# Feed-forward blocks of 512 tokens in (n2, n1) order in place of 376-token blocks, with the mixing stages placed to deadlines

## The chip, the cores and the metric

One core of a Trainium2 chip runs the kernel. The metric is the device time of the program in microseconds (us). The kernel before takes 980.5 us (three runs, 980.26 to 980.66).

Ratios are the mean time of one kernel's runs over that of the other's runs of the same rounds, so they are not quite the ratio of the medians that are quoted.

## The reference

```python
def _attn_ref(x, filt_r, filt_i):            # x: 8 batches x 3008 positions x 256 channels
    X = np.fft.rfft(x, axis=1)
    Y = X * (filt_r + 1j * filt_i)[None]
    return np.fft.irfft(Y, n=x.shape[1], axis=1)

def _moe_ref(x, w_gate, w_val, w_out):       # x: 24064 tokens x 256; d_ff = 1536
    return (np.maximum(x @ w_gate, 0.0) * (x @ w_val)) @ w_out
```

The output is the second function applied to the first, with the eight batches laid end to end. The row of the output for position s of batch b is 3008 b + s.

## The kernel before

The Fourier transform of length 3008 = 94 x 32 is done in stages. A position is s = 32 n1 + n2, with n1 below 94 and n2 below 32. Per batch, 16 **items of A** transform over n1 (matmuls psA, then a write to memory, Abuf, and a gather into `at`). 14 **items of B** transform over n2, multiply by the filter and transform back over n2 (psX, products tt and uu, psD, then a write to Dbuf and a load into dC). **Item C** (psY) finishes the inverse over n1 and yields yT, the input of the feed-forward. A and B of batch b + 1 are woven one by one into the feed-forward of batch b.

```python
    def items_b(b, junk=0):
        def fwd(g):
            psX = ps.tile([128, 2, D], FP32, tag=fft_tag(), name="psX")
            ...                                   # 2 matmuls
            nc.vector.tensor_tensor(tt, psX, Ftr[:, g:g + 2, :], op=ALU.mult)
            ...                                   # uu likewise, from psX and Fti
        def inv():
            psD = ps.tile([128, 2, D], FP32, tag=fft_tag(), name="psD")
            ...                                   # 4 matmuls
            nc.scalar.copy(st["dsb"][:, o:o + 2, :], psD)
        ...                                       # one item: fwd of one pair, inv of an earlier one

    def item_c(b, z, h):
        psY = ps.tile([128, W], FP32, tag=fft_tag(), name="psY")      # W = 376
        for j in range(4):
            nc.tensor.matmul(psY[:, j * N1:(j + 1) * N1],
                             dCs[b, z][:, j, h * 128:(h + 1) * 128], M1, start=True, stop=True)
        dst = yTs[b, z][:, h]
        src = psY.rearrange("p (b a) -> p a b", a=N1)
        ...                                       # copy: ScalarE for h == 0, VectorE for h == 1

    def gv(blk, ft, prods):                       # gate and value of 128 of the 1536 features
        ...                                       # 4 matmuls of W columns into psV and psG
        nc.scalar.copy(vsb, psV[:, :W])
        nc.vector.scalar_tensor_tensor(prod, in0=psG[:, :W], scalar=0.0, in1=vsb,
                                       op0=ALU.max, op1=ALU.mult)

    def o_part(blk, s, prods):                    # output tiles of 128, 128 and 120 tokens
        ...                                       # 3 matmuls of 256 columns, psO
        if s in (7, 11):
            n = 2 if s == 7 else 1
            osb = fs.tile([128, 2, D], FP32, tag="osb", bufs=3)
            nc.scalar.copy(osb[:tw, :n], psO[:tw, :n])
            r0 = b * S + (t + 1 - n) * 128 * NZ + z
            nc.sync.dma_start(_ap(out, r0 * D, [[NZ * D, tw], [128 * NZ * D, n], [1, D]]),
                              osb[:tw, :n])
    ...
    turn["tags"] = ("fft",)                       # psA, psX, psD, psY share ONE tag: 2 psum tiles
    for bi, blk in enumerate(blocks):             # 64 blocks: batch b, group z of four n2
        ...                                       # A from step 5 (20 in batch 0), B from step 35 (51), every 2nd
        for ft in range(NFT):                     # 12 "steps" of a block
            gv(blk, ft, prods)
            if prev is not None:
                o_part(prev[0], ft, prev[1])
            for f in side.get(z * NFT + ft, ()):  # the items of A and B, loads
                f()
            if ft in (6, 10) and bi + 1 < len(blocks):
                item_c(*blocks[bi + 1], 0 if ft == 6 else 1)
```

Psum is the memory that the matmuls write. The kernel keeps eight tiles in it: two each for psV, psG and psO, and two for the tag `fft`.

## Time and profile before

| | before |
|---|---|
| time, median of 3 | 980.53 us |
| span of the profiled run | 978.5 us |
| TensorE (PE) busy | 960.5 us, 98% |
| feed-forward stretch: first psV to the end of the last output matmul | 60.7 to 974.9 us |
| PE waits within that stretch | 0.7 us |

From the page of the kernel before: busy time of each engine, then groups of instructions (line, engine, what it writes and reads, shape, count, then busy us, mean ns of one, idle us before them and what ended it) and output transfers (count, KB each, us from issue to landing).

```profile
span 978.5 us, 18320 instructions
...
PE 960.5 (98%) x6814; PEld 663.3 (68%) x6816; DVE 577.1 (59%) x1046; ACT 556.6 (57%) x1191; POOL 51.4 (5%) x85
...
L365 PE MATMUL psO<-WoT,prod 128*128 128x256 bf16 (+1 forms) x2304 | 375.0, 273 | 0.0
L345 PE MATMUL psV<-yT,WvT 128*128 128x376 bf16 x1536 | 370.4, 322 | 0.7 <-ACT yT L334 0.4
...
L328 PE MATMUL psY<-M_90,dC 96*128 96x94 bf16 x512 | 42.3, 204 | 0.0
...
out_dram<-osb SPq DMA_DIRECT2D x64, 256.0 KB, 2.3
...
out_dram<-osb SPq DMA_DIRECT2D x64, 120.0 KB, 1.9
```

The waits of PE inside the feed-forward stretch (total us, times, longest), all of them:

```profile
PE psV L345 <- ACT yT L334: 0.4, 1, 0.4
PE psV L345 <- DVE yT L336: 0.3, 1, 0.3
```

And the stretch view: length, then busy us of PE, its weight loads, VectorE, ScalarE, GpSimd, then granted clock and DMA.

```profile
60.70:974.90 914.20, 913.84 (x6608) 641.08 (x6607) 549.68 (x1000) 535.46 (x1154) 22.19 (x43) 1.00 0.37 102
```

So PE is never free for 914 us. The mean of 322 ns for a matmul is not its cost, since matmuls overlap. The cost is the distance from one start to the next. By the chain of waits it is 159.3 ns for 376 columns, 109.2 for 256 and 42.0 for 94, which is columns / 2.4 GHz plus 2.5 ns.

I take the twelfth of a block as a step, measure from its first psO matmul to the next step's, and subtract the sum of its matmuls at those costs. In the kernel before, no step is more than 0.2 us over that sum. This is worked out from the starts of the instructions in the trace, and I call it the excess of a step.

### The profile page before, as it was taken

How to read it: one execution, taken by the hardware profiler on the slowest of the kernel's cores; microseconds unless marked ns; L12 is line 12 of the kernel's file. 1: busy time of each engine (PE TensorE's matmuls, PEld its weight loads, DVE VectorE, ACT ScalarE, POOL GpSimd, SP SyncE). 2: the span in 40 equal slices, each digit the busy share in tenths (PEclk: the TensorE clock that was granted, in tenths of full speed). 3: DMA queues.
4: the chain of work that ended last, by engine and by line, in shares of the span. 5: the costliest groups of instructions: out<-in, count | busy, mean ns of one | idle time of the engine just before them, and what ended most of it. 6: DMA issues, size and time to landing. Idle time of an engine off the chain costs nothing.

```text
span 978.5 us, 18320 instructions
## 1 busy us (share of the span) xinstructions
PE 960.5 (98%) x6814; PEld 663.3 (68%) x6816; DVE 577.1 (59%) x1046; ACT 556.6 (57%) x1191; POOL 51.4 (5%) x85
## 2 busy tenths in 40 slices
PE   8699999999999999999999999999999999999998
PEld 2355677667775677757776577765777567777776
DVE  4543486448753586536854378543875449655554
ACT  3245666555655565555655556555665555655554
POOL 4520000000000000000000100001000000000000
PEclk9899999999999999999999999999999999999999
DMA  9993824192413814155231652318332241411111
GB/s 263 211 258 106 228 61 119 49 246 68 132 38 101 203 52 130 32 160 147 76 114 32 172 137 84 97 44 226 83 108 65 64 114 54 129 33 33 32 33 48
DMA packets 96825, 107.20 MB, mean 110 GB/s; under 512 B 6212, under 2 KB 85508, under 8 KB 95108
## 3 DMA queue, kind: packets, MB, share of 16 engines
q1 hardware_dynamic: 87760, 78.97, 29.1%
q0 software_dynamic: 8576, 25.86, 10.4%
q8 instruction: 53, 0.87, 0.4%
q10 hardware_dynamic: 400, 1.20, 0.3%
q14 instruction: 36, 0.29, 0.1%
HBM read 59.31 MB, written 49.81 MB: 112 GB/s over the span
## 4 chain that ended last, share of the span: by engine, by line
PE 95%; DMA 3%; POOL 1%; DVE 0%; ACT 0%; issue 0%; POOLq 0%; ACTq 0%
PE psO L365 26%; PE psV L345 25%; PE psG L345 25%; PE psA L243 11%; PE psY L328 2%; PE psX L274 2%; PE psD L294 2%; PE psD L293 2%; PE psJ L382 1%; DMA XF_89<-in_x_dram 1%; DMA at<-Abuf_71 1%; DMA XF_88<-in_x_dram 1%; DMA Abuf_71<-asb 1%; POOL uu L281 0%; DVE tt L277 0%
## 5 line engine op out<-in xcount | busy, mean ns | idle before, releaser
L350 DVE SCALAR_TENSOR_TENSOR prod<-psG,vsb 128x376 bf16<-128x376 f32 x768 | 421.4, 550 | 357.4 <-ACT vsb L348 348.3
L348 ACT CAST vsb<-psV 128x376 bf16<-128x376 f32 x768 | 363.5, 473 | 210.0 <-PE psV L345 209.3
L365 PE MATMUL psO<-WoT,prod 128*128 128x256 bf16 (+1 forms) x2304 | 375.0, 273 | 0.0
L345 PE MATMUL psV<-yT,WvT 128*128 128x376 bf16 x1536 | 370.4, 322 | 0.7 <-ACT yT L334 0.4
L345 PE MATMUL psG<-yT,WgT 128*128 128x376 bf16 x1536 | 369.8, 322 | 0.0
L365 PEld LDWEIGHTS <-prod 128*128 128x128 bf16 (+1 forms) x2304 | 246.1, 110 | 89.9
L345 PEld LDWEIGHTS <-WgT 128*128 128x128 bf16 x1536 | 149.7, 97 | 95.7 <-issue 0.9
L345 PEld LDWEIGHTS <-WvT 128*128 128x128 bf16 x1536 | 143.2, 98 | 66.9 <-issue 54.9
L246 ACT CAST asb<-psA 96x512 bf16<-96x512 f32 x128 | 74.4, 582 | 101.6 <-PE psA L243 100.5
L296 ACT CAST dsb<-psD 128x512 bf16<-128x512 f32 x96 | 56.0, 587 | 50.1 <-PE psD L294 48.7
L370 ACT COPY osb<-psO 128x512 f32<-128x512 f32 (+1 forms) x128 | 61.6, 481 | 19.9 <-PE psO L365 13.9
L277 DVE TENSOR_TENSOR tt<-psX,Ftr 128x512 bf16<-128x512 f32 x96 | 65.4, 682 | 10.4 <-PE psX L274 10.3
L243 PE MATMUL psA<-XF_89,WA 128*96 128x512 f32 x128 | 65.0, 592 | 1.4 <-DMA XF_89<-in_x_dram 1.4
L243 PE MATMUL psA<-XF_88,WA 128*96 128x512 f32 x128 | 65.1, 593 | 0.5 <-DMA XF_88<-in_x_dram 0.5
L283 DVE TENSOR_TENSOR uu<-psX,Fti 128x512 bf16<-128x512 f32 x90 | 61.3, 681 | 0.0
L294 PE MATMUL psD<-uu,I2u 128*128 128x256 bf16 x192 | 47.4, 274 | 2.9 <-POOL uu L281 2.8
L293 PE MATMUL psD<-tt,I2t 128*128 128x256 bf16 x192 | 47.7, 274 | 0.0
L328 PEld LDWEIGHTS <-dC 96*128 96x128 bf16 x512 | 35.8, 97 | 14.8 <-issue 12.0
L274 PE MATMUL psX<-at,F_91 128*128 128x256 bf16 x192 | 37.4, 277 | 6.4 <-DMA at<-Abuf_71 6.4
L328 PE MATMUL psY<-M_90,dC 96*128 96x94 bf16 x512 | 42.3, 204 | 0.0
L336 DVE CAST yT<-psY 128x376 bf16<-128x376 f32 x64 | 34.6, 541 | 12.5 <-PE psY L328 12.5
L334 ACT CAST yT<-psY 128x376 bf16<-128x376 f32 x64 | 30.2, 472 | 20.0 <-PE psY L328 20.0
(47 smaller groups left out, 201.3 us busy)
## 6 DMA issues: line engine op xcount, KB each, us to landing
out_dram<-osb SPq DMA_DIRECT2D x64, 256.0 KB, 2.3
XF_88<-in_x_dram POOLq DMA_DIRECT2D x20, 512.0 KB, 7.2
XF_89<-in_x_dram POOLq DMA_DIRECT2D x20, 512.0 KB, 6.5
out_dram<-osb SPq DMA_DIRECT2D x64, 120.0 KB, 1.9
XF_88<-in_x_dram SPq DMA_DIRECT2D x6, 256.0 KB, 5.2
XF_89<-in_x_dram SPq DMA_DIRECT2D x3, 512.0 KB, 8.1
Abuf_71<-asb SPq DMA_DIRECT2D x4, 384.0 KB, 5.3
at<-Abuf_71 SPq DMA_DIRECT2D x4, 384.0 KB, 6.1
```

What stands on the lines that cost most here:

```text
L243: nc.tensor.matmul(psA[0:NROW], WA[:, :NROW], XF[c * NC2 // NX2][:, o:o + 512], start=True, stop=True)
L246: nc.scalar.copy(dst, psA[0:NROW])
L277: nc.vector.tensor_tensor(tt, psX, Ftr[:, g:g + 2, :], op=ALU.mult)
L283: nc.vector.tensor_tensor(uu, psX, Fti[:, g:g + 2, :], op=ALU.mult)
L293: nc.tensor.matmul(psD[:, i], I2t[:, g + i, :], tt[:, i], start=True, stop=False)
L294: nc.tensor.matmul(psD[:, i], I2u[:, g + i, :], uu[:, i], start=False, stop=True)
L328: nc.tensor.matmul(psY[:, j * N1:(j + 1) * N1], dCs[b, z][:, j, h * 128:(h + 1) * 128], M1, start=True, stop=True)
L345: nc.tensor.matmul(pt[:, :W], w[:, h, ft * 128:(ft + 1) * 128], yt[:, h, :], start=(h == 0), stop=(h == 1))
L348: nc.scalar.copy(vsb, psV[:, :W])
L350: nc.vector.scalar_tensor_tensor(prod, in0=psG[:, :W], scalar=0.0, in1=vsb, op0=ALU.max, op1=ALU.mult)
L365: nc.tensor.matmul(psO[:tw, t % 2], prods[ft][:, t * 128:t * 128 + tw], WoT[:, ft, :], start=(ft == 0), stop=(ft == NFT - 1))
L370: nc.scalar.copy(osb[:tw, :n], psO[:tw, :n])
```

## The change

The intent: with matmuls of 512 columns, a width that psA already has, 47 blocks of 512 tokens pay the 2.5 ns less often than 64 of 376, and all output tiles are full ones (2,256 output matmuls instead of 2,304). As 3008 is no multiple of 512, blocks cross batches and tokens are taken in the order n2, then n1. A batch now lasts about 70 steps instead of 96, and A, B and C are placed backward from the step at which a block first needs the batch.

```diff
-    W = S // NZ
+    W = 512
+    NB = B * S // W
...
+    def runs(t, n):                               # pieces of n tokens within one n2
+        o = 0
+        while o < n:
+            b, r = divmod(t + o, S)
+            n2, n1 = divmod(r, N1)
+            w = min(N1 - n1, n - o)
+            yield o, b, n2, n1, w
+            o += w
...
-        for j in range(4):
-            nc.tensor.matmul(psY[:, j * N1:(j + 1) * N1], ...
+        for (o, b, n2, n1, w) in runs(k * W, W):
+            nc.tensor.matmul(psY[:, o:o + w],
+                             dCs[b, n2 // 4][:, n2 % 4, h * 128:(h + 1) * 128], M1[:, n1:n1 + w],
+                             start=True, stop=True)
...
-            nc.sync.dma_start(_ap(out, r0 * D, [[NZ * D, tw], [128 * NZ * D, n], [1, D]]),
-                              osb[:tw, :n])
+            for tt in range(t0, t + 1):
+                for (o, b, n2, n1, w) in runs(blk * W + tt * 128, 128):
+                    nc.sync.dma_start(_ap(out, (b * S + n1 * N2 + n2) * D, [[N2 * D, w], [1, D]]),
+                                      osb[o:o + w, tt % 2])
...
+    LAST = 9
+    for b in range(1, B):
+        end = (b * S // W - 1) * NFT + LAST - 5
+        if b == 1:
+            s0, sb0 = 13, 33
+            every = [sb0 + i + i // 2 for i in range(14)]
+        else:
+            s0 = end - 54
+            every = [(s0 + 24 | 1) + 2 * i for i in range(14)]
+        for i, f in enumerate(items_a(b)):
+            at_step(s0 + i, f)
+        for c in range(4):
+            at_step(s0 + 6 + 4 * c, lambda b=b, c=c: load_at(b, c))
+        ...
+        for i, f in zip(every, items_b(b)):
+            at_step(i, f)
+        at_step(every[-1] + 1, lambda b=b: load_d(b))
...
-            if ft in (6, 10) and bi + 1 < len(blocks):
-                item_c(*blocks[bi + 1], 0 if ft == 6 else 1)
+            if ft in (LAST - 2, LAST + 1) and k + 1 < NB:
+                item_c(k + 1, 0 if ft < LAST else 1)
```

The permutation of n2 in the tables of the inverse is dropped with the old order, and the last block evicts its output tile by tile.

More of the change, by code (lines that the diff above doesn't have):

```diff
@@ L53, in _tables @@
     i2u = np.zeros((128, NG, 64))
-    perm = np.arange(N2) // 4 + 8 * (np.arange(N2) % 4)
-    perm = np.concatenate([perm, 32 + perm])
     for hg in range(48):
@@ L94, in _tables @@
         f2[lo + 16 * a, g] = f
-        i2t[rows, g], i2u[rows, g] = t[:, perm], u[:, perm]
+        i2t[rows, g], i2u[rows, g] = t, u
     tab = np.stack([f2, i2t, i2u], 1).reshape(128, 3, 2, NG // 2, 64).transpose(0, 2, 1, 3, 4)
@@ L119 @@
     NZ = 8
-    W = S // NZ
+    W = 512
+    NB = B * S // W
+    assert NB * W == B * S
     wa_h, m1_h, tab_h = _tables()
@@ L320, with item_c @@
     yTs = {}
-    def item_c(b, z, h):
+    def runs(t, n):
[6 more added lines that the diff above has]
+            o += w
+    def item_c(k, h):
         if h == 0:
-            yTs[b, z] = sb.tile([128, 2, N1, 4], BF16, tag="yT", bufs=3, name="yT")
+            yTs[k] = sb.tile([128, 2, W], BF16, tag="yT", bufs=3, name="yT")
         psY = ps.tile([128, W], FP32, tag=fft_tag(), name="psY")
-        for j in range(4):
-            nc.tensor.matmul(psY[:, j * N1:(j + 1) * N1],
-                             dCs[b, z][:, j, h * 128:(h + 1) * 128], M1,
+        for (o, b, n2, n1, w) in runs(k * W, W):
+            nc.tensor.matmul(psY[:, o:o + w],
+                             dCs[b, n2 // 4][:, n2 % 4, h * 128:(h + 1) * 128], M1[:, n1:n1 + w],
                              start=True, stop=True)
-        dst = yTs[b, z][:, h]
-        src = psY.rearrange("p (b a) -> p a b", a=N1)
+        dst = yTs[k][:, h]
         if h == 0:
-            nc.scalar.copy(dst, src)
+            nc.scalar.copy(dst, psY)
         else:
-            nc.vector.tensor_copy(dst, src)
+            nc.vector.tensor_copy(dst, psY)
     def gv(blk, ft, prods):
-        yt = yTs[blk].rearrange("p h a b -> p h (a b)")
+        yt = yTs[blk]
         psV = ps.tile([128, 512], FP32, tag="psv", name="psV")
@@ L356, in o_part @@
     def o_part(blk, s, prods):
-        b, z = blk
-        t = s // 4
-        tw = min(128, W - t * 128)
-        if s in (0, 8):
+        t = s // 3
+        if s in (0, 6):
             ost["ps"] = ps.tile([128, 2, D], FP32, tag="pso", name="psO")
         psO = ost["ps"]
-        for ft in range((s % 4) * 3, (s % 4) * 3 + 3):
-            nc.tensor.matmul(psO[:tw, t % 2], prods[ft][:, t * 128:t * 128 + tw], WoT[:, ft, :],
+        for ft in range((s % 3) * 4, (s % 3) * 4 + 4):
+            nc.tensor.matmul(psO[:, t % 2], prods[ft][:, t * 128:(t + 1) * 128], WoT[:, ft, :],
                              start=(ft == 0), stop=(ft == NFT - 1))
-        if s in (7, 11):
-            n = 2 if s == 7 else 1
+        last = blk == NB - 1
+        if s in (5, 11) or last and s % 3 == 2:
+            t0 = t if last else t - 1
             osb = fs.tile([128, 2, D], FP32, tag="osb", bufs=3)
-            nc.scalar.copy(osb[:tw, :n], psO[:tw, :n])
-            r0 = b * S + (t + 1 - n) * 128 * NZ + z
-            nc.sync.dma_start(_ap(out, r0 * D, [[NZ * D, tw], [128 * NZ * D, n], [1, D]]),
-                              osb[:tw, :n])
+            nc.scalar.copy(osb[:, t0 % 2:t % 2 + 1], psO[:, t0 % 2:t % 2 + 1])
+            for tt in range(t0, t + 1):
+                for (o, b, n2, n1, w) in runs(blk * W + tt * 128, 128):
+                    nc.sync.dma_start(_ap(out, (b * S + n1 * N2 + n2) * D, [[N2 * D, w], [1, D]]),
+                                      osb[o:o + w, tt % 2])
     junk = pro.tile([128, 512], BF16, tag="junk", bufs=1)
@@ L429 @@
     for h in range(2):
-        item_c(0, 0, h)
+        item_c(0, h)
     prologue.close()
@@ L434, with at_step @@
     turn["tags"] = ("fft",)
-    blocks = [(b, z) for b in range(B) for z in range(NZ)]
-    prev = None
-    for bi, blk in enumerate(blocks):
-        b, z = blk
-        if z == 0 and b + 1 < B:
-            side = {}
-            def at_step(s, f):
-                side.setdefault(s, []).append(f)
-            s0 = 5 if b else 20
-            for i, f in enumerate(items_a(b + 1)):
-                at_step(s0 + i, f)
-            for c in range(4):
-                at_step(s0 + 7 + 4 * c, lambda b=b, c=c: load_at(b + 1, c))
-            if b + 2 < B:
-                at_step(s0 + 19, lambda b=b: load_x(b + 2, nc.gpsimd))
-            sb0 = (s0 + 30) | 1
-            for i, f in enumerate(items_b(b + 1)):
-                at_step(sb0 + 2 * i, f)
-            at_step(sb0 + 31, lambda b=b: load_d(b + 1))
-        elif z == 0:
-            side = {}
+    side = {}
+    def at_step(s, f):
+        side.setdefault(s, []).append(f)
+    LAST = 9
[11 more added lines that the diff above has]
+            at_step(s0 + 6 + 4 * c, lambda b=b, c=c: load_at(b, c))
+        if b + 1 < B:
+            at_step(s0 + 17, lambda b=b: load_x(b + 1, nc.gpsimd))
+        for i, f in zip(every, items_b(b)):
+            at_step(i, f)
+        at_step(every[-1] + 1, lambda b=b: load_d(b))
+    prev = None
+    for k in range(NB):
         prods = []
         for ft in range(NFT):
-            gv(blk, ft, prods)
+            gv(k, ft, prods)
             if prev is not None:
                 o_part(prev[0], ft, prev[1])
-            for f in side.get(z * NFT + ft, ()):
+            for f in side.get(k * NFT + ft, ()):
                 f()
-            if ft in (6, 10) and bi + 1 < len(blocks):
-                item_c(*blocks[bi + 1], 0 if ft == 6 else 1)
-        prev = (blk, prods)
+            if ft in (LAST - 2, LAST + 1) and k + 1 < NB:
+                item_c(k + 1, 0 if ft < LAST else 1)
+        prev = (k, prods)
     for s in range(NFT):
```

## The prediction

> **What bounds the kernel.** TensorE: PE 960.5 of 978.5 us (page). From 60.7 us (feed-forward begins) to 974.9 us it is busy 913.84 of 914.20 us (stretch view); the waits show 0.7 us of PE stalls there. So only less PE work, or new stalls, change the time. DVE (59%) and ACT (57%) have room.
>
> **Cost of one matmul.** From the chain of waits: 159.3 ns for 376 columns, 109.2 for 256, 42.0 for 94: columns / 2.4 GHz plus 2.5 ns, as the Trainium skill says ("TensorE: Matmul & The Clock Gate", the 56 ns section); this trace agrees. The model gives 912.8 us for the 914.2 us above.
>
> **PE work (estimates from these durations).**
> - gate/value: 3072 x 159.2 = 489.1 us becomes 2256 x 215.9 = 487.0: -2.1.
> - output: tiles of 128, 128, 120 become full ones; 2304 matmuls of 109.2 ns become 2256: -5.2.
> - item C: same columns, about 90 more matmuls: +0.2.
> About -7 us, all on the critical path, and the most the change can give (0.7%). The fewer, longer DVE and ACT instructions are off the path.
>
> **What it adds.**
> 1. Output transfers: 128 become about 440, 0.35 us of SP queue each: harmless. But the Trainium skill ("DMA: Bandwidth & Descriptors", how many engines) says a transfer uses the largest k <= 16 dividing its rows: 94 rows use 2 engines. No run here shows it yet. By that rule the two lowest engines get 6,704 of the 24,064 rows each, not 1,504. At about 50 ns a row (estimate: 2.3 against 1.9 us to landing, 16 against 8 rows per engine) that is 260 us more on them. The last two transfers leave 64 rows on one engine: tail +3 us.
> 2. Batch 1 is hurried. Last A item at step 28, first B item at step 33. In the trace this chain (A eviction, write, gather of at) took 6.2 us to the last gather's issue and 7.0 us to landing; five new steps of 1.3 us give 6.7. Stall of 4 to 6 us, possibly a clock dip. Last inverse item at step 52, C's need at step 55: psD to first dC took 6.9 us; 4.3 are there. Stall of 2 to 3.
> 3. Batches 2 to 7: last A to first B had 15.6 us, the gather just in time. Now 13.4 us; but the third gather goes out a step earlier, out of the fourth's way. Last psD to C: 8.2 us for 6.9. Margins near nothing: 0 to 1.5 us per batch, say 3 in all.
>
> **Sum.** 980.5 - 7 + 3 + 7.5 + 3 = 987; shaded down, since gathers spread out may land sooner: 981. Range 974 to 993. The change roughly cancels itself. Chances: faster by over 2% 0.02, within 2% 0.92, slower 0.06.
>
> **What would show it.** 216 ns per 512-column matmul in the chain, PE work of the feed-forward stretch near 906 us. PE waiting on at<-Abuf once near step 33 (4 to 6 us), psY on dC (2 to 3 us), then 0 to 1.5 us per batch. Output transfers of 94 rows landing in 4 us rather than 2; 5 to 7 us from the last PE instruction to the end, not 3.5. PE never waits for DVE or ACT.
>
> **What would make it wrong.** If gathers land in 5 us, stalls almost vanish: 974 to 976. If the two lowest engines saturate during the A stage, every batch stalls 3 us or more and the clock drops: 995 or more. If transfers spread over 16 engines whatever their rows, tail and contention go.

## More of the kernel before

From the timeline of the SP queue of the kernel before (start, us, line, what it issues): the last A write of batch 1 and the gathers behind it.

```profile
107.91 0.31 SPq L248 DMA_DIRECT2D Abuf_72<-asb  x1
108.28 4.94 SPq L261 DMA_DIRECT2D at<-Abuf_72  x2
```

The second of these two gathers had to wait for the receipt of the write of 107.91 us, and was issued at 112.9 us. The write was therefore received in about 5 us.

## The result, and the profile after

The changed kernel takes 1012.7 us (median of 4 runs, 1011.88 to 1013.46) against 980.6 us beside it: ratio 1.0324, 95% interval 1.0306 to 1.0342. It is 3.2% slower. The result is correct.

| | before | after |
|---|---|---|
| span of the profiled run, us | 978.5 | 1011.3 |
| PE busy, us | 960.5 | 956.4 |
| mean granted clock | 0.997 | 0.985 |
| first psV to start of last output matmul, us | 913.95 | 941.3 |
| start of last output matmul to the end, us | 3.8 | 7.8 |
| PE waits in the feed-forward stretch, us | 0.7 | over 25 |

From the page after, in the same form. No landing time could be read for these output transfers.

```profile
span 1011.3 us, 16206 instructions
...
PE 956.4 (95%) x5934; PEld 567.5 (56%) x6044; DVE 545.6 (54%) x825; ACT 522.2 (52%) x938; POOL 51.5 (5%) x85
...
L372 PE MATMUL psO<-WoT,prod 128*128 128x256 bf16 x2256 | 339.1, 274 | 3.2 <-ACT osb L378 2.5
...
L338 PE MATMUL psY<-M_90,dC 96*128 96x94 bf16 (+18 forms) x604 | 37.8, 199 | 14.9 <-ACT dsb L296 9.4
...
out_dram<-osb SPq DMA_DIRECT2D x72, 94.0 KB
```

The feed-forward stretch after, in the columns of the stretch view above:

```profile
62.20:1003.52 941.32, 909.38 (x5723) 545.08 (x5831) 518.37 (x779) 500.66 (x901) 21.82 (x43) 0.99 0.35 99
```

PE has less work, and 32 of the 941 us are not busy (a little of that may be matmul records that are missing from the trace). The waits of PE in that stretch, over 1 us:

```profile
PE psY L338 <- ACT dsb L296: 9.4, 14, 0.7
PE psX L274 <- DMA at<-Abuf_72: 7.1, 1, 7.1
PE psY L338 <- DMA dC<-Dbuf_80: 5.5, 1, 5.5
PE psO L372 <- ACT osb L378: 2.5, 2, 2.0
PE psX L274 <- DMA out_dram<-osb: 1.1, 1, 1.1
```

The first line is the largest, and it is a wait for ScalarE to empty a psum tile. One of its 14 cases, from the timeline of the changed kernel (start, us, engine, line, what; in brackets the idle time before it and what ended it):

```profile
273.46 0.38 PE L274 MATMUL psX<-at,F_91 128*128 128x256 bf16 x2
...
273.68 0.27 PE L293 MATMUL psD<-tt,I2t 128*128 128x256 bf16 x1
...
274.01 0.27 PE L294 MATMUL psD<-uu,I2u 128*128 128x256 bf16 x1
...
274.32 0.58 ACT L296 CAST dsb<-psD 128x512 bf16<-128x512 f32 x1 [0.94 <-PE psD L294]
274.62 0.68 DVE L283 TENSOR_TENSOR uu<-psX,Fti 128x512 bf16<-128x512 f32 x1
...
274.96 0.39 PE L338 MATMUL psY<-M_90,dC 96*128 96x50 bf16 x6 [0.67 <-ACT dsb L296]
```

This is a step in which a B item and item C meet. psX and psD take the two psum tiles of the tag. psY comes right behind and starts 0.06 us after dsb has emptied psD, that is 0.84 us later than the last psD matmul plus its own cost would allow. Summed over steps, the 14 steps with psX, psD and psY have a mean of 3.03 us for 2.19 us of matmuls. The other kinds of step (with A, with B alone, with C alone) fit the sum of their parts as well as before, other than at the waits listed.

The second line, followed through the chain of waits of the changed kernel (start, us, what was waited for or done): batch 1 from its last A item to its first B item.

```profile
110.72 8.28 DMA Abuf_72<-asb
...
119.01 4.83 DMA at<-Abuf_72
...
123.89 0.61 PE psX L274 x2
124.50 0.85 PE psV L354 x2
```

Two things stand in it. The A write needed 8.28 us to its receipt, not 5. (How the time divides between write and gather differs from run to run. In the profiles of experiments 1 and 2, which differ up to here in item C alone, the write took 5.6 and 7.6 us and the gather 7.2 and 5.2. From the write's issue to the first psX it was 12.8 to 13.2 us in all three, against 10.5 with the plain outputs of experiment 5.) And after 7.1 us of idle PE, two matmuls take 0.85 us instead of 0.43: the clock is at one half. The trace grants half the clock in two stretches of 6.83 us, around this wait and around the wait for dC, and once more from 1001.4 us, in the last block, to the end. The Trainium skill ("TensorE: Matmul & The Clock Gate", "What's actually happening") says that the clock falls to one half after at least one idle window of about 3.4 us; both waits are longer than that, and this trace agrees.

The SP queue at that place, after:

```profile
109.36 0.32 SPq L261 DMA_DIRECT2D at<-Abuf_72  x1
110.72 0.30 SPq L248 DMA_DIRECT2D Abuf_72<-asb  x1
112.02 3.56 SPq L381 DMA_DIRECT2D out_dram<-osb  x5
119.01 0.33 SPq L261 DMA_DIRECT2D at<-Abuf_72  x1
```

The wait of the SP queue for an A write of one batch (batch 3) in all, first before and then after (total us, times, longest):

```profile
SPq L261 <- DMA Abuf_74<-asb: 1.7, 1, 1.7
```

```profile
SPq L261 <- DMA Abuf_74<-asb: 22.8, 4, 9.5
```

The third line of the PE waits, by the chain: the last B item of batch 1 is at step 52, the load of dC at step 53, behind the five output transfers that are issued in that step.

```profile
163.06 0.27 SPq L381
...
164.49 0.44 SPq L381
...
165.04 5.59 DMA dC<-Dbuf_80
...
170.68 0.23 PE psY L338
```

The bill, in us, from the traces and the excess of steps:

| item | us |
|---|---|
| PE work: gate/value, output and item C at 2.4 GHz plus 2.5 ns each (761.5 to 754.3, estimate from counts) | -7.2 |
| 14 steps in which B and C meet | +11.9 |
| batch 1, steps 33 and 34: wait for `at`, half clock after it | +9.1 |
| batch 1, steps 55 and 56: wait for dC, half clock after it | +7.7 |
| batch 3, first B item | +1.3 |
| last block: psO waits for osb, osb for output transfers; half clock for the last 12 matmuls | +3.8 |
| short matmuls of item C in the other steps | +0.8 |
| after the last output matmul's start | +4.0 |
| feed-forward begins later (62.2 for 60.7; other runs of the same prologue lie between 60.7 and 63.0) | +1.5 |
| sum | 32.9 |
| measured difference of spans | 32.8 |

The last block's 3.8 us are the distance from the first to the last start of its last 52 output matmuls, 9.37 us, less their cost of 5.57. Its last twelve, from the timeline, take 2.64 us at half the clock:

```profile
1001.30 2.64 PE L372 MATMUL psO<-WoT,prod 128*128 128x256 bf16 x12 [2.00 <-ACT osb L378]
```

The 0.8 us of item C are what its steps without a wait exceed their sums by, 1.2 us, less 0.4 us in the kernel before. Experiment 11 shows the same loss at a larger size.

### The profile page after: what moved, and what is told of

Its sections match the earlier page's. It is cut to its first block, busy times and chain, and to the rows that moved or that the text cites. A ratio compares the mean times of both kernels' runs of the same rounds, so it can differ in the third digit from the quotient of the medians.

```text
span 1011.3 us, 16206 instructions
## 1 busy us (share of the span) xinstructions
PE 956.4 (95%) x5934; PEld 567.5 (56%) x6044; DVE 545.6 (54%) x825; ACT 522.2 (52%) x938; POOL 51.5 (5%) x85
## 4 chain that ended last, share of the span: by engine, by line
PE 88%; DMA 5%; ACT 2%; DVE 2%; issue 1%; POOL 1%; SPq 0%; ACTq 0%; POOLq 0%
PE psG L354 24%; PE psO L372 23%; PE psV L354 22%; PE psA L243 10%; PE psY L338 2%; PE psX L274 2%; PE psD L294 2%; PE psD L293 2%; DVE prod L359 1%; ACT vsb L357 1%; DMA XF_89<-in_x_dram 1%; ACT dsb L296 1%; DMA Abuf_72<-asb 1%; PE psJ L391 1%; DMA Abuf_71<-asb 1%
## 5 line engine op out<-in xcount | busy, mean ns | idle before, releaser
L359 DVE SCALAR_TENSOR_TENSOR prod<-psG,vsb 128x512 bf16<-128x512 f32 x564 | 389.8, 691 | 397.5 <-ACT vsb L357 381.0
L357 ACT CAST vsb<-psV 128x512 bf16<-128x512 f32 x564 | 331.1, 587 | 223.1 <-PE psV L354 140.6
L372 PE MATMUL psO<-WoT,prod 128*128 128x256 bf16 x2256 | 339.1, 274 | 3.2 <-ACT osb L378 2.5
L354 PE MATMUL psG<-yT,WgT 128*128 128x512 bf16 x1107 | 332.2, 380 | 4.2 <-issue 0.2
L354 PE MATMUL psV<-yT,WvT 128*128 128x512 bf16 x1041 | 318.3, 380 | 1.8 <-ACT yT L343 0.4
L372 PEld LDWEIGHTS <-prod 128*128 128x128 bf16 x2256 | 221.7, 98 | 147.9 <-issue 4.5
L354 PEld LDWEIGHTS <-WgT 128*128 128x128 bf16 x1128 | 110.3, 98 | 135.2 <-issue 2.8
L354 PEld LDWEIGHTS <-WvT 128*128 128x128 bf16 x1128 | 104.5, 98 | 66.4 <-issue 55.5
L338 PE MATMUL psY<-M_90,dC 96*128 96x94 bf16 (+18 forms) x604 | 37.8, 199 | 14.9 <-ACT dsb L296 9.4
L345 DVE CAST yT<-psY 128x512 bf16<-128x512 f32 x47 | 32.1, 684 | 17.3 <-PE psY L338 17.2
```

What stands on the lines that cost most here:

```text
L338: nc.tensor.matmul(psY[:, o:o + w], dCs[b, n2 // 4][:, n2 % 4, h * 128:(h + 1) * 128], M1[:, n1:n1 + w], start=True, stop=True)
L354: nc.tensor.matmul(pt[:, :W], w[:, h, ft * 128:(ft + 1) * 128], yt[:, h, :], start=(h == 0), stop=(h == 1))
L372: nc.tensor.matmul(psO[:, t % 2], prods[ft][:, t * 128:(t + 1) * 128], WoT[:, ft, :], start=(ft == 0), stop=(ft == NFT - 1))
```

## The experiments

Twelve kernels ran. "Saved" below is the difference to the 1012.7 us of the changed kernel; the medians of the kernel before moved by at most 0.6 us between the sets. The texts name some runs by label: e10_best is experiment 10, e11_best2 experiment 11.

### 1. Item C moved off the B items

```diff
-            if ft in (LAST - 2, LAST + 1) and k + 1 < NB:
+            if ft in (LAST - 1, LAST + 1) and k + 1 < NB:
```

> The changed kernel with item C's first half emitted at step 8 instead of step 7 of a block (second half at 10 as before), so it never shares a step with a B item (B items of batches 2 to 7 are at odd steps). Theory (psY takes one of the two psum tiles that psX and psD of the B item just before it still hold, so TensorE waits for their evictions, 0.84 us in 12 steps of batches 2 to 7 and once or twice in batch 1): those steps fall from 3.02 us to the 1.95 + 0.24 us of their parts, and the batch-1 wait for dC shrinks by one step; about 12 us saved, near 1000 us, ratio to before near 1.020. Rival (DVE or ACT are simply overloaded in the B stage): the same delay shows up in other steps, and less than 3 us are saved.

Measured: 1000.05 us (998.83 to 1000.67), ratio 1.0193. It saved 12.7 us. Of the steps that had all three of psX, psD and psY, one is left (batch 1, step 46, still 0.86 us over).

### 2. psY out of the shared psum tiles, item C left where it was

```diff
-        psY = ps.tile([128, W], FP32, tag=fft_tag(), name="psY")
+        psY = ps.tile([128, W], FP32, tag="psv", name="psY")
```

> The changed kernel with psY taken from the psum tag of psV instead of the tag shared with psX and psD; item C stays at step 7. Theory (the shared psum tiles): TensorE no longer waits there and the steps with B and C fall from 3.03 to about 2.2 us although ACT and DVE have just as much to do in them; 10 to 12 us saved, near 1001 us. Rival (ACT and DVE are overloaded in that step): psV or psG waits instead, less than 4 us saved.

Measured: 1001.82 us (1000.69 to 1003.61), ratio 1.0218; 10.9 us saved. The 14 steps still hold B and C and fall to a mean of 2.20 us for 2.19 us of matmuls. ScalarE and VectorE have as much to do in them as before. Of the waits of psY only the one for dC is left:

```profile
PE psY L338 <- DMA dC<-Dbuf: 5.6, 2, 5.4
```

So it is the psum tiles and not the load of the two engines.

### 3. The same collision put into the kernel before

```diff
-            if ft in (6, 10) and bi + 1 < len(blocks):
-                item_c(*blocks[bi + 1], 0 if ft == 6 else 1)
+            if ft in (7, 10) and bi + 1 < len(blocks):
+                item_c(*blocks[bi + 1], 0 if ft == 7 else 1)
```

> The kernel before, unchanged but for item C's first half, emitted at step 7 of a block instead of 6, so that in 13 or 14 places it comes right behind a B item. Theory (psY finds both psum tiles of the tag held by that B item's psX and psD): each of these steps becomes 0.6 to 0.85 us longer, with psY waiting for the eviction dsb; 8 to 12 us in all, near 990 us, ratio 1.009 to 1.012. Rival (the delay belongs to the 512-token blocks): no change, ratio within 0.002 of 1.

Measured: 992.04 us (991.79 to 992.22), ratio 1.0116; 11.5 us slower than the kernel before. Fourteen steps have an excess of 0.84 us each, 11.7 us. The wait is to the digit that of the changed kernel:

```profile
PE psY L328 <- ACT dsb L296: 9.4, 14, 0.7
```

The collision has nothing to do with 512 tokens. It comes with one digit: in the kernel before B items stand at odd steps and item C at even ones.

### 4. Batch 1's B items later and closer together

```diff
-            s0, sb0 = 13, 33
-            every = [sb0 + i + i // 2 for i in range(14)]
+            s0, sb0 = 13, 38
+            every = [sb0 + i for i in range(14)]
```

> The changed kernel with batch 1's B items one per step from step 38 instead of three per four steps or so from step 33. Theory (batch 1 is hurried: last A at 28, first B at 33): the 7.1 us wait of psX for the gather of at falls to about 1 us and the clock dip after it goes, 8 us saved; the wait for dC at step 55 stays within 2 us of 5.5, since the last B item is at step 51 instead of 52. About 1004 us. Rival (the whole chain of batch 1 is too long for 55 steps, so a stall only moves from psX to dC): less than 3 us saved.

Measured: 996.82 us (995.78 to 997.28), ratio 1.016; 15.9 us saved, twice what I expected. The wait for `at` is gone in batch 1, and so is most of the wait for dC (excess of 0.85 us in step 55 for 6.5), and there is no half clock in the feed-forward any more until its last 0.6 us. The load of dC now leaves at step 52, before the output transfers of step 53, while it stood behind them at 53. That order was not part of my expectation.

### 5. Outputs in the old way, wrong result on purpose

```diff
-            for tt in range(t0, t + 1):
-                for (o, b, n2, n1, w) in runs(blk * W + tt * 128, 128):
-                    nc.sync.dma_start(..., osb[o:o + w, tt % 2])
+            n = t + 1 - t0
+            nc.sync.dma_start(_ap(out, (blk * W + t0 * 128) * D, [[D, 128], [128 * D, n], [1, D]]),
+                              osb[:, t0 % 2:t0 % 2 + n])
```

> Wrong result on purpose: the changed kernel writes each 128-token tile to 128 consecutive rows, one transfer for two tiles as before, in the wrong order; all else equal. It gives the whole price of cutting outputs into runs. Theory: tail from the last TensorE instruction to the end 3.8 us instead of 7.8, no wait of ACT for output transfers in the tail (2.2 us), batch 3's 1.3 us and about 3 us of the wait for dC in batch 1 (which stands behind five output transfers) gone: 9 to 12 us saved, near 1002 us. Rival (the outputs hold up the loads of every batch): more than 15 us saved.

Measured: 997.82 us (996.26 to 1000.11), ratio 1.0177; 14.9 us saved, at the upper edge. The output is wrong, as intended. From the timeline of its SP queue, at the same place in batch 1:

```profile
111.00 0.30 SPq L248 DMA_DIRECT2D Abuf<-asb  x1
112.30 0.40 SPq L380 DMA_DIRECT2D out_dram<-osb  x1
116.03 0.32 SPq L261 DMA_DIRECT2D at<-Abuf  x1
```

The A write is received in 5.0 us, as in the kernel before. The excess of step 33 falls from 8.3 to 5.6 us and that of step 55 from 6.5 to 2.8 us; batch 3's 1.3 us are gone; from the last output matmul's start to the end 4.0 us remain, not 7.8. The half clock after the two waits is still there, for 3.41 us each.

### 6. Outputs cut so that they spread over the DMA engines

```diff
+                    for (c0, c1) in ((0, w // 16 * 16), (w // 16 * 16, w)):
+                        if c1 > c0:
+                            nc.sync.dma_start(... rows c0 to c1 of the run ...)
```

> The changed kernel with each output run cut into a piece whose rows are a multiple of 16 and a rest of 2 to 14 rows (result unchanged, about 780 transfers). Theory (runs of 94 and other 2 x prime rows go to two DMA engines and overload them): packets of output rows run 14 to 16 at once, not 2; the tail from the last TensorE instruction to the end falls from 7.4 to about 4 us, the waits of ACT for output transfers (2.5 us of TensorE time in the tail, 1.1 us in batch 3) vanish, the write of A in batch 1 lands in 5 us instead of 8.3; 8 to 11 us saved, near 1003 us. Rival (number of transfers and the SP queue matter, not the spread): slower than the changed kernel.

Measured: 1008.32 us (1007.55 to 1008.77), ratio 1.0278. It saved 4.4 us, half of what I expected. The spread did come. In a stretch of 350 us of the changed kernel, exactly two packets of output rows were in flight for 56 of the 146 us in which there were any, and 16 or more for 0.3 us; in this run two for 7 of 84 us, and 16 or more for 4 us (counted from the packet records of the two traces). But the number of transfers has a price of its own. The last A write of batch 1 in this kernel, and the last gather:

```profile
111.06 0.30 SPq L248 DMA_DIRECT2D Abuf<-asb  x1
112.36 8.19 SPq L383 DMA_DIRECT2D out_dram<-osb  x9
120.60 0.42 SPq L261 DMA_DIRECT2D at<-Abuf  x1
```

The nine output transfers now occupy the SP queue for 8.2 us, and the gather is issued at 120.6 us, no sooner than after the slow write. The chain names an earlier output transfer as what the queue waited for. In the last block, too, SP issues 22 outputs in 9.1 us, one after another without a pause. My tail of "about 4 us" stayed at 6.8.

### 7. The gathers of `at` in their old order

```diff
-            at_step(s0 + 6 + 4 * c, lambda b=b, c=c: load_at(b, c))
+            at_step(s0 + 6 + 4 * c + (c < 3), lambda b=b, c=c: load_at(b, c))
```

> The changed kernel with the first three gathers of at issued one step later, that is right after the next A write instead of before it, as in the kernel before; nothing else. Theory (the third gather, issued just ahead of the fourth A write, holds that write up: 8 to 10 us to its receipt instead of 5): the fourth write is received in about 5 us and the last gather is issued 3 to 5 us sooner, but then shares the DMA engines with the third; the psX wait in batch 1 falls from 8.3 us by 0 to 3 and batch 3's 1.3 us goes; total 0 to 4 us saved, 1008 to 1013 us. Rival (outputs on two engines hold the write up): receipt stays at 8 to 10 us.

Measured: 1018.77 us (1018.34 to 1019.07), ratio 1.0389; 6 us slower than the changed kernel, a miss. The last A write of batch 1 and the last gather, from the timeline of its SP queue:

```profile
110.23 0.30 SPq L248 DMA_DIRECT2D Abuf<-asb  x1
116.27 1.74 SPq L261 DMA_DIRECT2D at<-Abuf  x1
```

The first half of the theory held. From the issue of the last A write to the issue of the last gather it took 6.0 us here, for 8.3 in the changed kernel. In batches 2, 4, 5 and 6 it took 4.8 to 5.0 us, for 5.0 to 8.7. Only batch 3 stayed slow (8.2 for 9.9). But the last gather itself became slower: in batch 1, 9.0 us from its issue to psX, for 4.9. So the excess of step 33 grew to 10.1 us, and batches 2 to 6 wait for their gathers (0.5 to 2.0 us). The order of the gathers in the change was the better one for the whole. The slow write is in part the doing of the third gather just ahead of it, but not of that alone: with the same order and plain outputs it is gone (experiment 5).

### 8. Experiments 1, 4 and 6 together

> All three edits: item C at step 8, output runs in multiples of 16, batch 1's B at steps 38 to 51. If the three causes are separate and complete, what remains is the gain of 7 us of TensorE work: 975 us, up to 979 with a wait of 1 to 3 us for dC in batch 1; ratio to before 0.994 to 0.998. If something else costs time in the 512-token blocks, over 983 us.

Measured: 982.67 us (981.87 to 982.95), ratio 1.0016. Of the 32 us, 30 are gone, but not the last seven. Left were 1.7 us in two steps of batch 1 where B and C still meet (now 44 and 46), 1 us at first B items, and 6.8 us after the last output matmul's start.

### 9. The token order of before in blocks of 512

Tokens go in groups of four n2 again (token 4 n1 + j of a group), so that a tile is cut only at a group's end: 217 transfers in the trace, and 8 to 16 engines for each by the rule of the divisor.

```diff
-            n2, n1 = divmod(r, N1)
-            w = min(N1 - n1, n - o)
+            z, q = divmod(r, 4 * N1)
+            w = min(4 * N1 - q, n - o)
...
+            part = psY[:, o:o + w].rearrange("p (a b) -> p b a", b=4)
+            for j in range(4):
+                nc.tensor.matmul(part[:, j], dCs[b, z][:, j, h * 128:(h + 1) * 128],
+                                 M1[:, q // 4:(q + w) // 4], start=True, stop=True)
```

> The changed kernel with only its token order taken back: within a batch the 32 values of n2 come in 8 groups of 4, as before (token 4 n1 + j of a group), so output rows are a regular stride of 8 and a tile is cut only where it crosses a group: 216 transfers in place of 440, all of 8 to 16 engines by the rule of the divisor. Blocks stay at 512. Item C then has 880 short matmuls instead of 604 (+0.7 us) that write psum with a stride. Result correct. Theory (the runs of the new order cost 15 us, the 512-token block itself nothing): within 2 us of the run with outputs in plain order, 996 to 1000 us. Rival (blocks that cross groups bring the cost by themselves): within 4 us of the changed kernel, 1008 us or more.

Measured: 1017.97 us (1016.49 to 1019.72), ratio 1.0376. Neither theory. The waits went as expected (excess of step 33 5.3 us, of step 55 2.4 us, 4.1 us at the end), but item C became slow, as the next run shows by itself.

### 10. All causes removed, first try

Experiment 9 with item C at steps 8 and 10 from psV's tag, and batch 1's B items at 38 to 51.

> All causes removed at once: 512-token blocks, the token order of the kernel before, item C at steps 8 and 10 with psY in psV's psum tag, batch 1's B items at steps 38 to 51. If the three causes are all there is, what is left is the gain of TensorE work, 7.2 less 0.7 us for the extra short matmuls: 974 to 976 us, ratio to before 0.993 to 0.996. If the 512-token block has a cost that I have not found, 979 us or more.

Measured: 998.35 us (998.04 to 999.48), ratio 1.0178. No wait over 0.5 us is left in its feed-forward stretch other than 1.0 us for osb at the end, and yet it takes 930.6 us. The steps with item C exceed the sum of their parts by about 21 us. The matmuls write psum with a step of four elements here. Started back to back, those of 94 columns follow each other in 65 ns on average instead of 41: about 41 after the first of a group, mostly 73 to 81 after the others.

### 11. The same without the stride

```diff
-            part = psY[:, o:o + w].rearrange("p (a b) -> p b a", b=4)
-                nc.tensor.matmul(part[:, j], dCs...
+            m = w // 4
+                nc.tensor.matmul(psY[:, o + j * m:o + (j + 1) * m], dCs...
...
+        for (o, b, z, q, w) in runs(k * W, W):    # the eviction puts (n2, n1) in order
+            dst = yTs[k][:, h, o:o + w].rearrange("p (a b) -> p a b", b=4)
+            src = psY[:, o:o + w].rearrange("p (b a) -> p a b", b=4)
```

> The run before this one (e10_best) lost 22 us in item C alone, its matmuls writing psum with a stride of 4 elements. Here each group's part is written without a stride, (n2, n1) in psum, and put in order by its eviction, 2 to 3 evictions per half in place of one. All else as in e10_best. If the stride was what cost, the steps with item C fall back to the sum of their parts and the feed-forward stretch to about 908 us, 7 us less the 0.7 for the extra matmuls under the kernel before: 974 to 977 us, ratio to before 0.993 to 0.997. If the count of short matmuls cost, it stays above 990 us.

Measured: 980.71 us (980.18 to 981.96), ratio 1.0006, interval 0.9993 to 1.002. The stride was what cost. The group of 94-column matmuls of item C, in the run before (with the stride) and in this one (without):

```profile
L342 PE MATMUL psY<-M,dC 96*128 96x94 bf16 x144 | 17.4, 275 | 0.0
```

```profile
L342 PE MATMUL psY<-M,dC 96*128 96x94 bf16 x144 | 11.8, 203 | 0.0
```

It missed its 974 to 977 us all the same: its feed-forward stretch takes 913.75 us, as long as before. The steps with item C are still about 5 us over the sum. The cuts make many matmuls of 2 to 54 columns, and these follow each other at 25 ns however few their columns are. The Trainium skill ("TensorE: Matmul & The Clock Gate", "Wait — 56ns, not 53.3ns?") states this floor of about 25 ns; this trace agrees, with 25 ns at every width from 2 to 52. (In experiment 12, where such matmuls stand singly, it is 29 to 30 ns; why was not looked into.) By columns / 2.4 GHz plus 2.5 ns they would need 3 to 24 ns. Sixteen matmuls of each even width from 2 to 52, at the difference, make 4.7 us (estimate).

### 12. The order of the change, with its causes removed

The changed kernel with item C at steps 8 and 10 from psV's tag, batch 1's B items at 38 to 51, and output runs cut only where an engine would get more than 12 rows: 600 transfers, the fullest engine getting 1,760 rows by the rule of the divisor. The last tile has its own eviction tile, and the cut-off rests of the last block leave from ScalarE's queue.

```diff
+                    k = max(i for i in range(1, 17) if w % i == 0)
+                    cut = w if w // k <= 12 else w // 16 * 16
+                    for i, (c0, c1) in enumerate(((0, cut), (cut, w))):
+                        if c1 > c0:
+                            eng = nc.scalar if last and i else nc.sync
+                            eng.dma_start(... rows c0 to c1 of the run ...)
```

> The changed kernel with its own token order, item C at steps 8 and 10 with psY in psV's psum tag, batch 1's B items at steps 38 to 51, and output runs cut at a multiple of 16 rows only where one engine would get more than 12 (600 transfers; the heaviest engine gets 1,760 rows, not 6,704); the last tile evicts into a tile of its own and the rests of the last block go out from ACT's queue. In this order item C needs only 604 matmuls. The feed-forward stretch should take 908 to 911 us (before: 914), the tail 4 to 6 us (before: 3.8): 976 to 979 us, ratio to before 0.995 to 0.999. If item C's short matmuls are not what ate the gain of e11_best2, it is no faster than that run (980.7).

Measured: 977.42 us (977.03 to 978.2, 6 runs) against 980.63: ratio 0.9968, interval 0.9955 to 0.9982. Its result is correct, and it beats both kernels, by 0.3% and 3.5%. The feed-forward stretch takes 910.0 us (914.0 before), and all its PE waits are:

```profile
PE psO L372 <- ACT osb L382: 1.6, 2, 1.1
PE psV L354 <- ACT yT L343: 0.4, 1, 0.4
PE psD L293 <- DVE uu L283: 0.3, 1, 0.3
PE psV L354 <- ACT vsb L357: 0.2, 1, 0.2
```

By the excess of steps, the 3.2 us that are missing from the 7.2 are 1.9 in the last block, 0.8 in the steps with item C's short matmuls and 0.5 in one B step that waits for uu.

This run also bears on the slow A write. From the issue of the last A write of a batch to that of the last gather, in us:

| | transfers | batch 1 | batches 3 to 6 |
|---|---|---|---|
| changed kernel | 440, runs | 8.3 | 5.6 to 9.9 |
| experiment 4 | 440, runs | 5.7 | 8.1 to 9.7 |
| experiment 6 | 784, spread | 9.5 (SP queue busy) | 5.2 to 8.3 |
| experiment 8 | 784, spread | 9.3 (SP queue busy) | 5.1 to 6.0 |
| this run | 600, spread | 6.2 | 5.0 to 5.2 |
| experiment 5 | plain outputs | 5.0 | 4.8 to 5.2 |

With more transfers than the changed kernel, but spread ones, the write of this run is hardly slower than with plain outputs. This points to the load on two engines, more than to the number of transfers, as what holds the write up; the number is paid on the SP queue (experiment 6). These runs differ in other edits too, so it is not shown by itself.

## Why the prediction was wrong

The prediction said 981 us, 974 to 993. The time was 1012.7.

**Right: what the change can give.** PE work falls by 7.2 us by the counts; the kernel of experiment 12, with the stalls taken away, shows 4 of these in the feed-forward stretch, and its trace shows where the other 3 went.

**Wrong: "PE never waits for DVE or ACT."** This is the step that failed most: psY waits for the eviction dsb, 0.84 us in 14 steps, 11.9 us in all. I read from the page that ScalarE and VectorE are busy for under 60% and concluded that their instructions are "off the path". I did not ask which psum tile the next matmul needs. The diff shows item C moving from step 6 to step 7 while B stays at odd steps. Experiment 3 reproduces the loss in the kernel before (11.7 us), and experiment 2 removes it without moving anything.

**Wrong in size: the stalls of batch 1, "4 to 6 us" and "2 to 3".** Measured were 9.1 and 7.7 us. The gaps that I worked out from the steps were right as far as they went: with outputs in plain order (experiment 5) the two stalls are 5.6 and 2.8 us. Missing were two terms. The outputs in runs add 2.7 and 3.7 us to these two. The dips of the clock, which I called possible and gave no time, add about 2.

**Wrong in place: the runs of the outputs, counted as "tail +3 us" and "harmless" on the SP queue.** The rule of the divisor (the Trainium skill, "DMA: Bandwidth & Descriptors", "How many engines (k)") held: in the last 5.1 us of output packets exactly two rows were in flight for 3.65 us, each taking 46 ns. The tail was +4.0 us, with 3.8 more in the last block. But the whole price was 14.9 us (experiment 5), since A writes, gathers and loads of dC stand behind these transfers. I had put 260 us more on two engines into the text and charged only the tail for it. I thought that a gather earlier in the queue would help the last one; experiment 7 shows that it does (4.9 us for the last gather in batch 1, not 9.0). But where outputs are cut into runs, the A write behind that earlier gather is received in up to 9.9 us rather than 5.

**Wrong: the shading from 987 to 981.** There was no measurement behind it. The sum of my own terms was nearer.

**Held: the other batches.** "0 to 1.5 us per batch, say 3 in all" measured 1.3 us, in one batch.

What is not settled: how the slow A write divides between the loaded engines, the gather just ahead of it (experiment 7) and the number of transfers. Spreading the rows removes most of it in experiments 8 and 12, but not in all batches of experiment 6.

## What to carry to other kernels

On an engine that is never idle, a step's cost is the sum of its parts only as long as every matmul finds a free psum tile. Before moving one stage by a step, list which stages share a buffer tag and whether they will now meet in the same step. When a change of token order cuts transfers, charge their cost to every transfer that stands behind them on the queue, not only to the end of the kernel; and compare the gain with the size of the stalls that a hurried first batch can bring, the drop of the clock included.

## What the Trainium skill lacked or had wrong

- "PSUM — Partial Sum Buffer" ("Specifications (TRN2)") says that any non-contiguous access pattern slows matmuls significantly, but gives no figure. Here 94 columns took 65 ns from start to start with a step of four fp32 elements and 41 ns without; about 16 us (estimate from the excess of steps) over the 880 matmuls of item C (experiments 10 and 11).
- "DMA: Bandwidth & Descriptors" gives the rule for the number of engines, and it fits (two rows in flight, 46 ns each). It has no figure for what a transfer on two engines does to those behind it: here the receipt of a 384 KB write went from 5.0 us to 8.3 (batch 1) and 9.9 us (batch 3).
- The same page ("Issuing engines are not separate DMA queues") says that issuing from several engines only saves the issue time, "usually small relative to the DMA itself". With many transfers of few rows the issue time is not small: 0.3 to 0.6 us each, and in the last block of experiment 6 SP issues 22 outputs in 9.1 us without a pause, while the 46 ns that a row takes on its engine give about 2.2 us for a whole run of 94 rows on two engines (estimate).
- "TensorE: Matmul & The Clock Gate" was right in what was used of it: 2.5 ns per matmul, the floor of 25 ns, and half the clock after waits of 5.5 and 7.1 us (6.83 us each time in the changed kernel). It names an idle window of about 3.4 us as the condition; in experiment 5 a wait of 2.4 us for dC was enough for 3.41 us at half the clock, which began 0.6 us after PE had resumed.
